# An unused 128 B tile behind the constants of a Mamba-2 scan with a mixer, and a decay tile 128 B longer

## The chip, the cores and the metric

The kernel runs on one core of one Trainium2 chip. The metric is device time in microseconds of one execution. In the profile PE is TensorE (matrix products), PEld its weight loads, DVE is VectorE, ACT is ScalarE, POOL is GpSimd and SP is SyncE, which here only issues DMAs. SBUF is the on-chip memory: 128 partitions, and a tile has the same byte address in each of them. PSUM holds the results of matrix products.

## What is computed

The first half is a scan over chunks (Mamba-2 SSD): for each of 4 batches and 8 heads, a sequence of 768 steps with head size 32 and state size 16.

```python
for c in range(nc):                       # chunks along the sequence
    cum = cumsum(log(a)[chunk])
    M = einsum('bhin,bhjn->bhij', Cc, Bc) * exp(cum_i - cum_j) * causal
    y[chunk] = M @ xc + einsum('bhin,bhnd->bhid', Cc, state) * exp(cum)
    state = exp(sum) * state + einsum('bhjn,bhjd->bhnd', Bc * decay_from_j, xc)
```

Its output, laid out as (batch 4, sequence 768, model 256), goes through a mixer: `u = x + ((x.T @ U) @ V).T` with rank 32 along the sequence, and `out = u + relu(u @ w_ch1) @ w_ch2` with 1024 inner channels. Inputs x, a, B and C are fp32; U, V, w_ch1 and w_ch2 are 64-bit floats, which the kernel loads as pairs of 32-bit words and converts on the chip.

## The kernel before

**Work and order.** The scan is cut into 12 pairs: 4 batches by 3 blocks of 256 steps. The mixer works per batch, on three blocks of 256 positions each. There is no loop that sets the order: `PLANS`, a list of words written out by hand, names every step (`g` gram, `m` and `M` mask, `s` state, `u` update, `i`, `n`, `j` the scan's outputs, `p`, `x`, `a` the low-rank part, `S`, `f`, `e`, `h`, `d` the two large products), and `follow` (L963) issues them in that order, with `manual_schedule` (L156), so that each engine takes its instructions as they are written. The mixer of one batch runs between the scan steps of a later one.

**The large products.** A product in full precision is split into three cheaper ones: an operand is written as a rounded part ("near"), a rest ("far") and a combination of both. `split` (L761) makes the tiles `u0`, `u1` and `u2` from a block of the mixer's input; `first` (L796) and `second` (L803) multiply them by the weights `w1[0]`, `w1[1]`, `w1[2]`; `second` and `third` (L814) write the three parts of the rectified result into tiles called `words`; `down` (L854) multiplies these by `w2[0]`, `w2[1]`, `w2[2]`, and `rows` (L822) does the same for the last block with the roles of the two operands exchanged. All of them issue their products through one line, L772. The first two blocks of batch 0 use plain fp32 products instead (`plain`, L783). DVE operations go through a recording helper and all have line L169.

**Loads.** `load_bc` (L199) and `load_x` (L212) fetch the inputs of the scan, and `load_words` (L241) the weights, all issued on SP by `begin` (L194, L195). The tile `bc` holds, for each head, B of two blocks of 128 steps and then C for 256 steps. A partition gets B in runs of 64 B, C in runs of 128 B and x in runs of 128 B.

**Where tiles lie.** Tiles come from four SBUF pools opened at L123 to L126: `const` (constants, weights and the decay tables), `raw` (the tiles `bc`, `x` and `words`), `att` (the scan's tiles) and `mix` (the mixer's). They lie behind each other in this order, and within a pool the tags lie in the order of their first use, every tile rounded up to 32 B. So a longer tile pushes all that lies behind it. The addresses of the built program, in bytes from the start of a partition, and their remainder modulo 256:

| tiles (pool) | before | modulo 256 |
|---|---|---|
| w10 to w12, w1f, w20 to w22 (const) | 20608 and on | 128 |
| ident and most other constants (const) | 77952 and on | various |
| bc, x, words (raw) | 86720, 94912, 103104 | 192 |
| BC, T, Cm (att): scaled B and C, and their transposes | 152256, 156352, 162496 | 192 |
| own (att), 1408 B | 168640 | 192 |
| bd, M, S, Sm (att) | 170048, 172096, 180288, 182336 | 64 |
| yT, ytok, pT, o, u0, u1, u2 (mix) | 185408 to 223296 | 64 |

The tile `own` is used once, in `keep` (L376), where DVE multiplies the logarithms of the decays by a mask and sums them. The tile `settled` (L457) is the last one of the `const` pool.

Of the kernel before, what the change touches and what calls it, by code (L numbers as in the profile page):

```python
# [10 lines left out]
FP32 = mybir.dt.float32  # L11
# [63 lines left out]
def kernel(  # L75
# [28 lines left out]
    P = 128  # L104
    NB, NH, S, D = x.shape
# [13 lines left out]
    Q = 32  # L119
# [3 lines left out]
    const = ctx.enter_context(tc.tile_pool(name="const", bufs=1))  # L123
    raw = ctx.enter_context(tc.tile_pool(name="raw", bufs=4))
    att = ctx.enter_context(tc.tile_pool(name="att", bufs=2))
# [17 lines left out]
    def bank(tag, *dims):  # L143
        t = psum.tile([P, *dims], FP32, tag=tag, name=tag, bufs=BANKS[tag])
        if fills[0]:
            idle(t if len(dims) == 1 else t.rearrange(
                {2: "p a b -> p (a b)", 3: "p a b c -> p (a b c)"}[len(dims)]), fills[0])
        fills[0] = 0
        return t
# [101 lines left out]
    own = {}  # L251
# [124 lines left out]
    def keep(bs, tag="w"):  # L376

        n = bs.stop - bs.start
        d = bank(tag, n, NC, NH)
        nc.tensor.matmul(out=d, lhsT=after, rhs=la[:, bs], start=True, stop=False,  # L380
                         skip_group_check=True)
        nc.tensor.matmul(out=d[:, :, :NC - 1], lhsT=onward, rhs=la[:, bs, 1:], start=False,
                         stop=True, skip_group_check=True)
        nc.scalar.activation(FD[:, bs], d, AF.Exp)

        d = bank(tag, n, NC, 2, NH)
        nc.tensor.matmul(out=d[:, :, :, 0], lhsT=middle, rhs=la[:, bs], start=True, stop=True,
                         skip_group_check=True)
        for m, sl in ((high, slice(0, NC - 1)), (low[0], slice(1, NC))):
            nc.tensor.matmul(out=d[:, :, :NC - 1, 1], lhsT=m, rhs=la[:, bs, sl], start=False,  # L390
                             stop=True, skip_group_check=True)
        J = 2 * NC - 1
        own = att.tile([P, NB, J, NH], FP32, tag="own", name="own", bufs=1)[:, :n]
        vector.tensor_tensor(
            out=own, in0=d.rearrange("p b c v h -> p b (c v) h")[:, :, :J],
            in1=mine[:, None, None, :].to_broadcast(own.shape), op=ALU.mult)
        vector.tensor_reduce(out=kept[:, bs], in_=own, axis=mybir.AxisListType.X, op=ALU.add)
        nc.scalar.activation(kept[:, bs], kept[:, bs], AF.Exp)
# [56 lines left out]

    st = {}
    settled = const.tile([P, 1], FP32)  # L457
    behind = {"turn": 0, "first": []}
    yT, ytok = {}, {}

    def prep(k, c=0, n=2):

        b, q = pairs[k]
        if "BC" not in st.setdefault(k, {}):
            st[k]["BC"] = att.tile([P, 2, 2, NH, N], FP32, tag="BC", name="BC")
        for g in [slice(4) if n == 2 else slice(c, c + 1) if c < 2 else slice(2, 4)]:
            part = st[k]["BC"].rearrange("p i c h n -> p (i c) h n")[:, g]
            vector.tensor_tensor(
                out=part, in0=bc_sb[k].rearrange("p h i c n -> p (i c) h n")[:, g],
                in1=F[:, b, q].rearrange("p h i c -> p (i c) h")[:, g, :, None].to_broadcast(  # L470
                    part.shape), op=ALU.mult)
# [479 lines left out]
    def ytokens_of(k, v):  # L951
# [4 lines left out]
                 j=crossed, y=yout, t=ytokens, L=load, Q=lambda k, c: prep(k, c, 1),  # L956
                 E=lambda k, c: decayed(k, c, 1), O=ytokens_of,
                 V=lambda k, c, v: turn(k, c, 1, "wx"[v // 2], vector if v % 2 else None))
    whole = dict(c=convert, R=refined, A=lambda i: decays(every_batch, "w", [i]),
                 K=lambda n: keep(every_batch, "z"), F=fill,  # L960
                 v=lambda n: spread())

# [53 lines left out]
```

## Time and profile before

| what | value |
|---|---|
| time of 3 runs, median (lowest to highest) | 225.8 us (225.74 to 226.55) |
| the profiled execution's own time | 225.21 us |
| its span, first to last instruction | 223.5 us |
| granted TensorE clock | 0.999 |
| busy: PE, PEld, DVE, ACT, POOL | 214.7, 192.8, 163.7, 122.5, 6.5 us |
| DMA | 69345 packets, 14.61 MB |

The profile shows one execution. A group's row gives the engine, the operation, what it writes and reads with the shape, how many there are, their busy time and the mean duration of one. Matrix products are pipelined, so one lasts longer than the distance to the next; the distance is what counts for the time, and the timeline of PE shows it: rows with a start, a length and a number of products, where a row's start and the next one's start lie as far apart as its products take. The chain of waits follows the work that ended last back from the last instruction.

### The profile page before, as it was taken

The numbers are of one execution on the slowest core, as the hardware profiler recorded it, in microseconds if no ns is written. First come the engines' busy times: TensorE is split into PE (matmuls) and PEld (weight loads), VectorE is DVE, ScalarE is ACT, GpSimd is POOL, SyncE is SP. The second block draws the span as 40 slices with busy tenths as digits, with TensorE's granted clock in tenths as the row PEclk, the third lists the DMA queues.
The fourth block names the chain that finished last, engine by engine and source line by source line (L and its number), as shares of the span: only waits on it lengthen the run. The fifth ranks groups of instructions, "written<-read, shape, count | busy, mean of one in ns | idle before, by whom it ended". The sixth has DMA issues, their size and how long they took to land.

```text
span 223.5 us, 7716 instructions
## 1 busy us (share of the span) xinstructions
PE 214.7 (96%) x3374; PEld 192.8 (86%) x3374; DVE 163.7 (73%) x341; ACT 122.5 (55%) x275; POOL 6.5 (3%) x22
## 2 busy tenths in 40 slices
PE   7977899899999999999999999999999999999994
PEld 5846567678889988989999997899998999999994
DVE  3489899999997979688189748948881694917541
ACT  2335774879548655674675351678332357545431
POOL 4023000000000000000000000000000000000000
PEclk9999999999999999999999999999999999999999
DMA  5977899989850005032015010200000000000142
GB/s 86 130 124 130 157 153 229 236 218 154 113 78 4 0 3 94 3 66 81 6 23 73 3 47 3 100 3 1 3 0 3 3 0 0 4 0 0 50 141 94
DMA packets 69345, 14.61 MB, mean 65 GB/s; under 512 B 63616, under 2 KB 67520, under 8 KB 69312
## 3 DMA queue, kind: packets, MB, share of 16 engines
q1 hardware_dynamic: 69312, 14.13, 32.5%
q8 instruction: 26, 0.43, 0.8%
q14 instruction: 7, 0.06, 0.1%
HBM read 10.98 MB, written 3.15 MB: 63 GB/s over the span
## 4 chain that ended last, share of the span: by engine, by line
PE 84%; SPq 8%; DMA 4%; DVE 2%; issue 1%; DVEq 0%
PE x L772 36%; PE z L772 28%; SPq L195 8%; DMA words<-in_moe_w_ch_dram 2%; PE w L730 2%; PE x L652 2%; PE w L891 2%; PE x L527 2%; PE w L701 2%; PE z L676 2%; PE x L741 2%; PE x L676 2%; DMA words<-in_moe_U_dram 1%; PE w L495 1%; PE w L562 1%
## 5 line engine op out<-in xcount | busy, mean ns | idle before, releaser
L169 DVE SCALAR_TENSOR_TENSOR words<-words 128x512 fp32r<-128x512 f32 (+6 forms) x60 | 39.5, 673 | 8.8 <-PE x L772 4.3
L772 PE MATMUL x<-words,w 128*128 128x256 f32 x288 | 39.5, 282 | 0.0
L772 PEld LDWEIGHTS x<-words,w 128*128 128x128 f32 x288 | 35.9, 188 | 1.0 <-issue 0.8
L772 PE MATMUL z<-u,w 128*128 128x256 f32 x240 | 34.4, 282 | 0.0
L772 PE MATMUL x<-u,w 128*128 128x256 f32 x240 | 33.9, 283 | 0.0
L772 PEld LDWEIGHTS z<-u,w 128*128 128x128 f32 x240 | 30.5, 188 | 0.5 <-issue 0.2
L772 PEld LDWEIGHTS x<-u,w 128*128 128x128 f32 x240 | 30.4, 189 | 0.4 <-issue 0.2
L777 ACT ACTIVATE z<-z 128x512 f32<-128x512 f32 (+1 forms) x24 | 13.7, 572 | 15.8 <-PE z L772 15.6
L777 ACT ACTIVATE x<-x 128x512 f32<-128x512 f32 (+1 forms) x27 | 15.3, 572 | 10.4 <-PE x L772 10.3
L772 PE MATMUL z<-words,w 128*128 128x256 f32 x144 | 19.5, 282 | 0.0
L772 PEld LDWEIGHTS z<-words,w 128*128 128x128 f32 x144 | 17.8, 188 | 0.3 <-issue 0.2
L169 DVE SCALAR_TENSOR_TENSOR words<-x,words 128x512 fp32r<-128x512 f32 x20 | 13.7, 686 | 4.8 <-ACT words L812 4.7
L169 DVE SCALAR_TENSOR_TENSOR words<-z,words 128x512 fp32r<-128x512 f32 x20 | 13.7, 686 | 3.1 <-ACT words L812 3.1
L812 ACT ACTIVATE words<-x 128x512 fp32r<-128x512 f32 x20 | 11.9, 600 | 6.5 <-PE x L772 6.5
L812 ACT ACTIVATE words<-z 128x512 fp32r<-128x512 f32 x20 | 11.8, 597 | 5.1 <-PE z L772 5.0
L594 ACT ACTIVATE Sm<-S,slot 128x128 f32<-128x128 f32 (+1 forms) x18 | 6.1, 389 | 14.4 <-DVE S L169 14.4
L169 DVE SCALAR_TENSOR_TENSOR S<-S,kept,w 128x64 f32<-128x64 f32 x40 | 11.2, 280 | 2.5 <-PE w L562 0.8
L169 DVE TENSOR_TENSOR BC<-bc,F 128x512 f32<-128x512 f32 (+2 forms) x18 | 8.7, 509 | 3.2 <-ACT F L372 2.6
L169 DVE TENSOR_TENSOR yT<-x,yT 128x384 f32<-128x384 f32 (+1 forms) x15 | 9.2, 616 | 2.3 <-PE x L772 2.0
L169 DVE TENSOR_TENSOR M<-x,causal 128x256 int32<-128x256 int32 x24 | 9.0, 418 | 2.4 <-PE z L527 2.4
L169 DVE TENSOR_TENSOR u<-yT,u 128x512 fp32r<-128x512 f32 x10 | 6.9, 688 | 5.2 <-ACT u L766 5.2
L652 PE MATMUL z<-T,Sm 32*64 32x64 f32 x180 | 9.7, 236 | 0.3 <-DVE settled L169 0.3
(146 smaller groups left out, 390.6 us busy)
## 6 DMA issues: line engine op xcount, KB each, us to landing
words<-in_moe_w_ch_dram SPq DMA_DIRECT2D x7, 512.0 KB, 6.0
x<-in_x_dram SPq DMA_DIRECT2D x24, 128.0 KB, 3.4
out_dram<-o SPq DMA_DIRECT2D x8, 256.0 KB, 2.2
bc<-in_B_dram SPq DMA_DIRECT2D x24, 64.0 KB, 3.4
bc<-in_C_dram SPq DMA_DIRECT2D x12, 128.0 KB, 3.3
out_dram<-words SPq DMA_DIRECT2D x3, 256.0 KB, 2.6
words<-in_moe_w_ch_dram SPq DMA_DIRECT2D x2, 256.0 KB, 4.5
out_dram<-o SPq DMA_DIRECT2D x2, 128.0 KB, 1.7
```

Source lines behind the costliest of these rows:

```text
L169: self.last = call(*args, **kwargs)
L195: op = nc.sync.dma_start(**kwargs)
L527: nc.tensor.matmul(out=g[r][cols, c], lhsT=s["T"][rows, 0, c, cols], rhs=s["Cm"][rows, :, :, ts(2 * c + p, Q)].rearrange("r v t i -> r v i ...
L594: nc.scalar.activation(s["Sm"][:, sl, v], s["S"][:, sl, ts(v, D)], AF.Copy, scale=slot[:, v, None])
L652: product = nc.tensor.matmul(out=y[r // 2][p][ts(r % 2, H), c], lhsT=own[ts(r, Q)], rhs=s["T"][ts(r, Q), 1, :, ts(2 * c + p, Q)].rearrange ...
L676: product = nc.tensor.matmul(out=y[n][p][ts(i, Q), c], lhsT=x_sb[k][half, c, h], rhs=s["M"][half, h // 2, c, h % 2], start=fresh(k, n, p, ...
L701: nc.tensor.transpose(out=t[:, c, g], in_=yT[b][:, g, ts(2 * q + c, P)], identity=ident)
L730: nc.tensor.matmul(out=p[ts(q, Q)], lhsT=U_sb[:, c], rhs=ytok[b][:, c, ts(q // 2, P)], start=(c == 0), stop=(c == NC - 1), skip_group_chec ...
L741: nc.tensor.matmul(out=h[q][:, :VS], lhsT=pT[rows], rhs=V4[rows], start=True, stop=True, skip_group_check=True)
L772: nc.tensor.matmul(out=t, lhsT=lhsT, rhs=rhs, start=start, stop=True, skip_group_check=True)
L777: nc.scalar.activation(t, t, AF.Copy, scale=1.0 + EPS)
L812: nc.scalar.activation(gs[j, i][0], t, AF.Relu, scale=NEAR)
```

## The change

One constant tile that nothing reads or writes is allocated behind `settled`, and `own` is allocated with 384 elements per partition (1536 B) in place of 352 (1408 B), of which the first 352 are used as before.

```diff
@@ keep
         J = 2 * NC - 1
-        own = att.tile([P, NB, J, NH], FP32, tag="own", name="own", bufs=1)[:, :n]
+        own = att.tile([P, 3 * P], FP32, tag="own", name="own", bufs=1)
+        own = own[:, :n * J * NH].rearrange("p (b j h) -> p b j h", b=n, j=J)
         vector.tensor_tensor(
             out=own, in0=d.rearrange("p b c v h -> p b (c v) h")[:, :, :J],
             in1=mine[:, None, None, :].to_broadcast(own.shape), op=ALU.mult)
@@
     st = {}
     settled = const.tile([P, 1], FP32)
+    gap = const.tile([P, Q], FP32)
     behind = {"turn": 0, "first": []}
```

In the built program the pool `raw` and, of `att`, BC, T, Cm and `own` start 128 B later than before; bd, M, S, Sm and the whole pool `mix` start 256 B later; `const` stays. Modulo 256, then, `raw`, BC, T, Cm and `own` go from 192 to 64, and everything else keeps its remainder. The list of instructions on every engine, their order, their semaphores, the slot that each tile takes and the PSUM addresses are the same in both programs.

## The prediction

> **What bounds the kernel now.** I read the page's busy times and chain first, since the change touches every engine's addresses and none of its instructions: what matters is which engine passes a longer operand on to the end.
>
> ```profile
> PE 214.7 (96%) x3374; PEld 192.8 (86%) x3374; DVE 163.7 (73%) x341; ACT 122.5 (55%) x275; POOL 6.5 (3%) x22
> ...
> PE 84%; SPq 8%; DMA 4%; DVE 2%; issue 1%; DVEq 0%
> ```
>
> TensorE is busy for 96% of the span and holds 84% of the chain; 36.0 and 28.2 points of that are the large products of L772. SP's issues and DMA make up 12% and lie at the start: in the chain's first 29.56 us SP issues B, C and x one behind the other (1.24 to 15.86 us), then come U (3.35 us) and a block of w1 (5.10 us). So there are two places where an address can cost time: the loads up to 30 us, and the pace of the large products after that. DVE and ACT are not on the chain to speak of, but would be with slower operands.
>
> **The change part by part.** It adds no instruction, wait or DMA and removes none. It moves tiles: `raw` (bc, x, words) and BC, T, Cm and own go from 192 to 64 modulo 256; bd, M, S, Sm and all of `mix` move by 256 B and keep their remainder. If a duration depended on the place of an operand, the trace of before would show it, since it holds both remainders already: tiles at 192, at 64, and constants at 128.
>
> *DVE and ACT.* Rows with the same operation and shape, at different remainders, by group with shapes kept apart:
>
> ```profile
> L169 DVE SCALAR_TENSOR_TENSOR words<-words 128x512 fp32r<-128x512 f32 x40 | 27.7, 692 | 8.8 <-PE x L772 4.3 <-PE z L772 3.1
> L169 DVE SCALAR_TENSOR_TENSOR u<-u,u 128x512 fp32r<-128x512 f32 x10 | 6.9, 692 | 1.4 <-PE z L772 1.1
> L169 DVE SCALAR_TENSOR_TENSOR w<-words,w 128x512 fp32r<-128x512 f32 x8 | 5.5, 692 | 0.3
> ```
>
> All operands at 192, all at 64, and a mix of 192 and 128: 692 ns each time. ACT's copies of 128x512 take 589 ns into o (64) and 594 to 611 ns into words (192, 4 of them): at most 22 ns by place, and not on the chain. I take 0 for DVE and ACT; the bound is 4 copies times 22 ns, 0.1 us either way.
>
> *Small products.* T, Cm and x are read in runs of 128 B at every multiple of 128 B from their start, so that a shift of 128 B exchanges the two halves of their products: as many start at 192 as before. 0. BC is read whole as weights of the transposes (L495, 276 ns each), as yT at 64 is (L701, 274 ns): 2 ns times 48, 0.1 us at most.
>
> *Large products.* The mean duration is 282 ns for x<-words and z<-u and 283 ns for x<-u, but the timeline shows that their distance is not one number:
>
> ```profile
> 117.79 1.07 PE L772 MATMUL z<-u,w 128*128 128x256 f32 x8
> 118.70 0.62 PE L772 MATMUL x<-u,w 128*128 128x256 f32 x4
> 119.15 1.57 PE L772 MATMUL z<-words,w 128*128 128x256 f32 x12
> 120.56 0.60 PE L701 MATMUL w<-ident,yT 128*128 128x128 f32 x4
> ```
>
> 8 with u take 118.70 - 117.79 = 0.91 us, 114 ns each; 12 with words take 120.56 - 119.15 = 1.41 us, 117.5 ns each. Over the trace there are 900 distances between neighbouring products of this kind with no wait in them: 247 of 113 or 114 ns, 653 of about 118 ns, a difference of 4.4 ns. With words streamed, 88% take 118 ns; with u streamed, 63%; with w2 streamed and words as weights, 12%. Relative to the weights at 128, words lies at +64, u at -64, and w2 against words at -64 too. After the change words would lie at -64, as u does. That is the one sign that speaks for an effect. Against it stand the exceptions:
>
> ```profile
> 212.13 1.98 PE L772 MATMUL z<-words,w 128*128 128x256 f32 x16
> 213.95 0.60 PE L891 MATMUL w<-ident,yT 128*128 128x128 f32 x4
> ```
>
> ```profile
> 150.33 2.52 PE L772 MATMUL x<-u,w 128*128 128x256 f32 x20
> 152.69 0.64 PE L772 MATMUL z<-u,w 128*128 128x256 f32 x4
> ```
>
> 16 with words take 1.82 us, 114 ns each, and 20 with u 2.36 us, 118 ns each; the same pair of u0 and w10 addresses comes back for other blocks with 113 ns one time and 118 ns another. So neither pace belongs to an address; it holds on for a stretch and changes where the streamed tile changes. I take 0. The bounds: all 653 steps of 118 ns brought to 113, 653 x 4.4 ns = 2.9 us less; the 247 others brought to 118, 1.1 us more. A rule of the Trainium skill bears on this: "SBUF — State Buffer", section "Who interferes with whom", says that TensorE and ScalarE never wait for anyone in SBUF; by it an address changes nothing in the pace, and the sum stays at 0, while by the rows above it could be -2.9 us.
>
> *Loads.* C's runs of 128 B start at 192 + 128, that is at 64 modulo 256 before, inside one block of 256 B; after, they start at 192 and reach over a border of 256 B, all of them. x's runs start at 192 and 64 by turns, before and after: half of them cross already. B's runs of 64 B never do. Time from issue to landing:
>
> ```profile
> x<-in_x_dram SPq DMA_DIRECT2D x24, 128.0 KB, 3.4
> ...
> bc<-in_B_dram SPq DMA_DIRECT2D x24, 64.0 KB, 3.4
> bc<-in_C_dram SPq DMA_DIRECT2D x12, 128.0 KB, 3.3
> ```
>
> x and C move 128 KB in 1024 runs each; half crossing or none differ by 0.1 us, so that all crossing costs 0.2 us at most. The packets say less still: 128 B ones take 13 ns each, from the 5th to the 95th percentile, those of x among them. Six of the 12 C loads are issued before 30 us, where SP is on the chain: 0 to 6 x 0.2 = 1.2 us. I take 0, by the packets. The weights' runs of 1024 B and more start off a border at 192 as at 64: 0. If the cover of PE's work went, the later six C loads (to 115.6 us) would add another 1.2 us; they are issued well ahead of use, and DVE waits 0.6 us in all for any bc.
>
> The sum is 0 on the profiled execution's 225.21 us (span 223.5 and 1.7 around it). That execution is 0.6 us under the median of the three, 225.8, and all four lie between 225.2 and 226.6; I forecast the median.
>
> **The rivals.**
>
> *Faster: words takes u's place at the weights, and its pace.* For it speaks the order 88, 63, 12% above and that a stretch with u at 114 ns turns to 118 ns with the first product of words, as at 119.15 us. If the 404 steps with words only took u's share, they would gain 404 x (0.88 - 0.63) x 4.4 ns = 0.4 us, hardly to be seen. If the distance of 113 ns then also held on from u to words, it would reach from all steps with words, 404 x 0.88 x 4.4 ns = 1.6 us, to all 653, 2.9 us: 222.9 to 224.2 us. It is beyond 0.5% if over 260 steps change. Against it: words at 114 ns and u at 118 ns in the same trace.
>
> *Slower: C's runs across a border of 256 B.* Its place is SP's chain up to 30 us, where transfers follow each other with DMA engines 80% busy over the first 30 us; the price is at most 0.2 us for each of six loads, 1.2 us: 227.0 us. It would be seen from 0.19 us each on. Against it stands x, which crosses with half its runs at the same 13 ns a packet. The Trainium skill has a rule for it: "DMA: Bandwidth & Descriptors", section "How a descriptor splits into AXI transactions", says that a descriptor goes out in transactions that start on 256 B borders, with bytes ahead of it moved for nothing. By that an unaligned C run would need 10 beats of 32 B in two transactions where it now needs 6 in one, if writes go as the reads that the page speaks of; the trace, with 13 ns for x's crossing and plain runs alike, does not show it.
>
> *Slower by the pace:* the stretches of 113 ns with u, or those of w2 with words (which goes to +64), are lost: up to 1.1 us, 226.9 us, for the same reason as above with the sign turned.
>
> *The change doesn't do what it says:* the shift could be lost in rounding. The addresses of the built program exclude it: 86720 becomes 86848, 185408 becomes 185664.
>
> **How the numbers follow.** No effect, 225.2 to 226.6 us: 0.60. Faster by the pace of the products: 0.24, of which 0.22 is beyond 0.5% (1.1 us, about what a measurement of this kernel can tell from no change). Slower by C's loads: 0.10, of which 0.09 beyond 0.5%. Slower by the pace: 0.06, about all of it near its end. So faster 0.22, same 0.64, slower 0.14. The predicted time is 225.8 us. The range takes the whole of no effect, about half of the faster case (from 223.8 us) and nearly all of the slower ones (to 227.0 us).
>
> **What would show it.** Right: the L772 rows keep 282 ns, the share of 118 ns distances stays near 653 of 900 with words near 88%, C lands after 3.3 us, the words block of w1 that the chain takes at 24.44 us starts there again. Faster: in PE's timeline the stretches with words have 114 ns. Slower: C's landing above 3.4 us and the first product of L772 on the chain, at 35.63 us now, later by as much as the span. Wrong altogether: a DVE or ACT row of 128x512 with another mean.

## The result and the profile after

The changed kernel takes 224.62 us (median of 21 runs, 222.74 to 226.01), the kernel before 225.74 us (21 runs, 224.42 to 227.81). The ratio is 0.9941, 95% interval 0.9916 to 0.9967: faster by 0.6%, 1.3 us. The forecast was no change; the range held the time. Here and below, ratios and intervals leave out the few executions that lie over 1.5% above the fastest of their kernel.

The two profiled executions last 225.21 and 223.32 us, with spans of 223.5 and 221.6 us. First the page of the changed kernel: busy times, and the chain by engine. L772 is L774 here, all lines behind L456 lie two further on.

```profile
PE 213.2 (96%) x3374; PEld 191.4 (86%) x3374; DVE 163.5 (74%) x341; ACT 122.3 (55%) x275; POOL 6.5 (3%) x22
...
PE 88%; SPq 7%; DMA 1%; DVE 1%; issue 1%; ACT 0%; DVEq 0%
```

DVE, ACT and POOL are where they were within 0.2 us; TensorE has lost 1.5 us of busy time with the same 3374 products. The groups of DVE with 128x512 elements, as the prediction showed them:

```profile
L169 DVE SCALAR_TENSOR_TENSOR words<-words 128x512 fp32r<-128x512 f32 x40 | 27.7, 692 | 8.5 <-PE x L774 4.1 <-PE z L774 3.0
L169 DVE SCALAR_TENSOR_TENSOR u<-u,u 128x512 fp32r<-128x512 f32 x10 | 6.9, 692 | 1.3 <-PE z L774 0.9
L169 DVE SCALAR_TENSOR_TENSOR w<-words,w 128x512 fp32r<-128x512 f32 x8 | 5.5, 692 | 0.3
```

Still 692 ns: in these rows the shift by 128 B changes nothing for DVE. The timeline of TensorE, at the same place in the order as the four lines of before:

```profile
117.07 1.07 PE L774 MATMUL z<-u,w 128*128 128x256 f32 x8
117.98 0.62 PE L774 MATMUL x<-u,w 128*128 128x256 f32 x4
118.43 1.53 PE L774 MATMUL z<-words,w 128*128 128x256 f32 x12
119.80 0.60 PE L703 MATMUL w<-ident,yT 128*128 128x128 f32 x4
```

12 with words now take 119.80 - 118.43 = 1.37 us, 114 ns each, where they took 117.5; u keeps 114. The stretch of 20 with u, 118 ns each before:

```profile
149.58 2.43 PE L774 MATMUL x<-u,w 128*128 128x256 f32 x20
151.85 0.62 PE L774 MATMUL z<-u,w 128*128 128x256 f32 x4
```

2.27 us, 113.5 ns each, though u has its old remainder. And near the end, where w2 is streamed and words are the weights, first before, then after:

```profile
218.49 1.07 PE L772 MATMUL x<-w,words 128*128 128x256 f32 x8
219.39 1.07 PE L772 MATMUL z<-w,words 128*128 128x256 f32 x8
```

```profile
216.51 1.10 PE L774 MATMUL x<-w,words 128*128 128x256 f32 x8
217.46 1.10 PE L774 MATMUL z<-w,words 128*128 128x256 f32 x8
```

8 in 0.95 us, 119 ns each, where they took 219.39 - 218.49 = 0.90 us, 112.5 ns each. So this kind went the other way. Of the 900 distances, 217 are longer than 114 ns, where 653 were; nearly all of these lie between 116 and 120 ns and are called the 118 ns pace below, those of 113 and 114 ns the 113 ns pace. The shares at 118 ns: words 22% (88% before), u 20% (64%), w2 with words 93% (17%). (The prediction's 63% for u and 12% for w2 count from 116 ns on, its 653 from 115.) Last, the loads, from issue to landing:

```profile
x<-in_x_dram SPq DMA_DIRECT2D x24, 128.0 KB, 3.8
...
bc<-in_B_dram SPq DMA_DIRECT2D x24, 64.0 KB, 3.6
bc<-in_C_dram SPq DMA_DIRECT2D x12, 128.0 KB, 4.3
```

C needs 1.0 us more, x 0.4 and B 0.2. The first large product of the chain begins at 36.07 us, 35.63 before.

The account of the 1.9 us between the spans: 0.44 us later into the large products (in this execution the granted TensorE clock also stood at half for 3.4 us from 24.3 us on, in that of before it did not); then 185.53 in place of 187.87 us, 2.34 less. Of these the 900 distances give 104.9 - 103.0 = 1.9 us. A stall of TensorE at 43.13 us, 0.65 us of "issue" in the chain of before, is missing after and gives about 0.9 us with what stood around it; the stretches of small products take 0.5 us more (40.3 in place of 39.8 us from the first large one on), in which there is one gap of 0.69 us between two products, at 141.31 us, that the trace of before lacks. The stall came back in the second profile of the same changed kernel (e8, 1.52 us at 46.46 us), so it belongs to an execution and not to the change.

### The profile page after: what moved, and what is told of

It is laid out like the page before. It is cut to its first block, busy times and chain, and to the rows that moved or that the text cites. A ratio compares the mean times of both kernels' runs of the same rounds, so it can differ in the third digit from the quotient of the medians.

```text
span 221.6 us, 7716 instructions
## 1 busy us (share of the span) xinstructions
PE 213.2 (96%) x3374; PEld 191.4 (86%) x3374; DVE 163.5 (74%) x341; ACT 122.3 (55%) x275; POOL 6.5 (3%) x22
## 4 chain that ended last, share of the span: by engine, by line
PE 88%; SPq 7%; DMA 1%; DVE 1%; issue 1%; ACT 0%; DVEq 0%
PE x L774 36%; PE z L774 28%; SPq L195 6%; PE x L654 3%; PE x L529 2%; PE w L732 2%; PE w L703 2%; PE w L893 2%; PE x L678 2%; PE z L678 2%; PE w L497 2%; PE x L743 2%; DMA words<-in_moe_U_dram 1%; PE w L564 1%; PE z L654 1%
## 5 line engine op out<-in xcount | busy, mean ns | idle before, releaser
L774 PE MATMUL x<-words,w 128*128 128x256 f32 x288 | 38.5, 280 | 0.0
L774 PEld LDWEIGHTS x<-words,w 128*128 128x128 f32 x288 | 35.0, 188 | 1.0 <-issue 0.8
L774 PE MATMUL z<-u,w 128*128 128x256 f32 x240 | 34.0, 281 | 0.0
L774 PE MATMUL x<-u,w 128*128 128x256 f32 x240 | 33.3, 281 | 0.0
L774 PEld LDWEIGHTS z<-u,w 128*128 128x128 f32 x240 | 30.1, 188 | 0.5 <-issue 0.2
L774 PEld LDWEIGHTS x<-u,w 128*128 128x128 f32 x240 | 29.9, 188 | 0.4 <-issue 0.2
L779 ACT ACTIVATE z<-z 128x512 f32<-128x512 f32 (+1 forms) x24 | 13.7, 572 | 15.4 <-PE z L774 15.2
L774 PE MATMUL z<-words,w 128*128 128x256 f32 x144 | 19.3, 281 | 0.0
L774 PEld LDWEIGHTS z<-words,w 128*128 128x128 f32 x144 | 17.6, 188 | 0.3 <-issue 0.2
L169 DVE SCALAR_TENSOR_TENSOR words<-x,words 128x512 fp32r<-128x512 f32 x20 | 13.7, 686 | 4.1 <-ACT words L814 4.1
L169 DVE SCALAR_TENSOR_TENSOR words<-z,words 128x512 fp32r<-128x512 f32 x20 | 13.7, 684 | 2.8 <-ACT words L814 2.8
```

Source lines behind the costliest of these rows:

```text
L169: self.last = call(*args, **kwargs)
L774: nc.tensor.matmul(out=t, lhsT=lhsT, rhs=rhs, start=start, stop=True, skip_group_check=True)
L779: nc.scalar.activation(t, t, AF.Copy, scale=1.0 + EPS)
```

## The experiments

Theory A: the pace of the large products is set by where the streamed tile starts against the weights, modulo 256 B; 64 (words before) holds it at 118 ns, 192 (u, and words after) leaves it free. With the weights at 128, a tile at 192 has the difference 64 and a tile at 64 the difference 192; for words, u and w2 the numbers below are differences, for bc and the other tiles they are addresses modulo 256. Theory B: the absolute start of the streamed tile sets it. Theory C: any shift does, or chance. Against the gain stands C's crossing of 256 B borders. "Pace" is below the number of the 900 distances that are longer than 114 ns, counted in the one profiled execution of each run; percentages are shares of such distances; the difference is (start of the streamed tile - start of the weights) modulo 256.

**e1, everything but the constants by 256 B.**

```diff
+    gap = const.tile([P, 64], FP32)      # behind settled; own as before
```

> The unused constant tile is 256 B and the decay tile has its old length: raw, att and mix all lie 256 B further, every remainder modulo 256 is that of the kernel before. Theory A (the pace of the large products is set by where the streamed tile starts against the weights, modulo 256): nothing changes, ratio 1.000 within 0.3%, about 650 of the 900 distances at 118 ns, words near 88%, C lands after 3.3 us. Theory C (any shift of the layout, or modulo 512, changes the pace): like the changed kernel, ratio near 0.994 and about 220 of 900.

Ratio 1.0002 (0.9966 to 1.0038). Pace 713 of 900, words 96%, u 70%; C lands after 3.1 us. A shift that keeps the remainders changes the time by less than 0.4% and leaves the pace near that of before: theory C falls, and modulo 512 with it.

**e2, the longer decay tile alone.** words stays at difference 64, u goes there from 192.

```diff
+        own = att.tile([P, 3 * P], FP32, tag="own", name="own", bufs=1)   # no gap
```

> Only the decay tile is longer, by 128 B: raw, BC, T and Cm stay at 192, while bd, M, S, Sm and mix (u among them) go from 64 to 192. Theory A: u now lies at +64 against the weights like words, so that u as well as words take 118 ns in 85% of the distances or more, over 750 of 900, about 0.6 us more than before, ratio 1.002 to 1.005; w2 streamed against words stays at 113 ns; C lands after 3.3 us. Theory C: the time and the pace move without regard to which tile moved, and words and u keep their difference.

Ratio 1.0039 (1.0007 to 1.0070). Pace 803: u 96% (64% before), words 88%, w2 with words 26%. The timeline of e2:

```profile
148.95 1.10 PE L773 MATMUL z<-u,w 128*128 128x256 f32 x8
149.89 0.63 PE L773 MATMUL x<-u,w 128*128 128x256 f32 x4
150.36 1.57 PE L773 MATMUL z<-u,w 128*128 128x256 f32 x12
151.77 2.40 PE L773 MATMUL x<-u,w 128*128 128x256 f32 x19
```

8 with u in 0.94 us and 12 in 1.41 us, 117.5 ns each: u takes on the pace of words when it takes on the difference. But 64 does not exclude 113 ns. One chain of e2 has it in u and words alike, up to its end at 128.49 us:

```profile
122.50 1.61 PE L773 MATMUL z<-u,w 128*128 128x256 f32 x12
123.95 1.52 PE L773 MATMUL z<-words,w 128*128 128x256 f32 x12
125.31 0.62 PE L773 MATMUL z<-u,w 128*128 128x256 f32 x4
```

12 with words take 125.31 - 123.95 = 1.36 us, 113 ns each.

**e3, the unused tile of 128 B alone.** words to 192, u to 64.

```diff
+    gap = const.tile([P, 32], FP32)      # own as before
```

> Only the unused constant tile of 128 B: raw, BC, T and Cm go to 64, and bd, M, S, Sm and mix (u among them) go to 192. Theory A: words at -64 has the 113 ns, u at +64 the 118 ns, the two exchange their parts: words under 40% at 118 ns, u over 80%, together 500 to 600 of 900, 0.2 to 0.7 us less by the pace, 0.4 us more by C's loads (landing 4.3 us as in the changed kernel), ratio 0.998 to 1.002. Theory C: words and u change alike.

Ratio 1.0087 (1.0054 to 1.0120), outside what was expected. Pace 749: u 96%, words 74% and not under 40%, w2 with words 31% though it lies at 64. So u is held at 64 again, but words at 192 gained little: most stretches of words follow one of u at 118 ns, and most of those stay there (18 of 22 that follow u without a break). The distances are 0.5 us longer in sum than before; the rest of the loss of 2.0 us is put down to C's crossing (landing 4.4 us), dearer than the 0.4 us that was allowed for it.

**e4, e11 and e14, the changed kernel with bc left at 192.** The unused tile lies between bc and x; words, u and weights have the addresses of the changed kernel, C does not cross.

```diff
         if k not in x_sb:
+            if not x_sb:
+                raw.tile([P, 32], FP32, tag="gap", name="gap", bufs=1)
             x_sb[k] = raw.tile([P, 2, NH, D], FP32, tag="x", name="x")
...
-    gap = const.tile([P, Q], FP32)       # of the changed kernel
```

> As the changed kernel, but the unused tile lies in raw between bc and x, so that bc alone stays where it was, at 192, and C's runs do not cross a border of 256 B. Theory A with a cost of C's crossing: pace as in the changed kernel (near 217 of 900 at 118 ns), C lands after 3.3 us and not 4.3, and the first large product comes 0.4 us earlier than in the changed kernel: ratio 0.991 to 0.993, ahead of both kernels. If crossing costs nothing and the later start has another reason: as the changed kernel, 0.994, with C's landing at 4.3 us.

> The kernel with bc left in place once more: words, u and weights have the addresses of the changed kernel, whose pace came back with 217 and 191 of 900, while this one had 523. Theory A with a pace at 192 that hangs on what went before in an execution: another number, anywhere from 190 to 550. If bc's place or the missing crossing of C sets it: 523 again within 60. The time: ratio 0.993 to 0.998.

> Words at 64 and bc at 192, next to the changed kernel on the same chip: by the two terms (pace 1 to 2 us less, no crossing) ratio 0.987 to 0.994, 0.4 to 1.2 us ahead of the changed kernel. If the crossing is covered: as the changed kernel within 0.3%.

Ratios 0.9959 (0.9930 to 0.9988), 0.9868 (0.9820 to 0.9916) and 0.9932 (0.9895 to 0.9968). C lands after 3.1, 3.2 and 3.2 us. Pace 523, 174 and 415 in the three profiles of one and the same kernel. So the difference 192 does not fix the pace; it leaves it open, and one execution has three times as many distances of 118 ns as another. e4 gained less than expected (0.991 to 0.993) and e11 more. This version is ahead of the kernel before: each interval lies below 1. In e4 that is not firm, since the mean of all its executions is 0.9992 of that of the kernel before (0.9877 in e11, 0.9937 in e14). On the chip that it shared with the changed kernel (e15) it was at 0.9932 against 0.9988, two intervals that overlap. The timeline of e11:

```profile
118.40 1.53 PE L775 MATMUL z<-words,w 128*128 128x256 f32 x12
119.77 0.60 PE L704 MATMUL w<-ident,yT 128*128 128x128 f32 x4
```

1.37 us for 12 with words, 114 ns each, as in the changed kernel.

**e5, the constants moved too.** The unused tile lies ahead of all constants: every absolute start moves by 128 B, the differences stay.

```diff
+    ahead = const.tile([P, 32], FP32)
     a_sb = const.tile([NB * NH * NC // 2, 2, P], FP32)
```

> The unused tile of 128 B lies ahead of all constants, so that everything moves by 128 B together: the weights of the large products go from 128 to 0, words from 192 to 64, u from 64 to 192, and their differences stay. Theory A (the difference sets the pace): the pace of the kernel before, u near 0.65 and words near 0.88 at 118 ns, about 650 to 710 of 900. Theory B (the absolute start of the streamed tile sets it): the exchange that the unused tile of 128 B behind the constants alone gave, u near 0.96 and words well below it. In both C crosses and lands after 4.3 us, 0.4 us lost at the start: ratio 1.001 to 1.005.

Pace 650, words 88%, u 64%, w2 with words 17%: the kernel before had 653 with 88, 64 and 17%. Theory B falls. The ratio is 1.0074 (1.0041 to 1.0106), more than expected. In the profile it lies ahead of the large products, which start at 38.81 us, with C at 4.1 us; but this execution also had half the clock for 17 us there, so the profile alone does not split the loss.

**e6, e7, e9 and e10, other differences.** The decay tile is the longer one; the unused tile has 192, 64, 160 and 96 B, which puts words and u alike at 128, 0, 96 and 32, and so at the differences 0, 128, 224 and 160.

```diff
+    gap = const.tile([P, 48], FP32)      # e6; 16 in e7, 40 in e9, 24 in e10
```

> Unused tile of 192 B and the longer decay tile: words, u and w1, w2 all start at 128, difference 0 in all three kinds of large products, w2 against words too. Theory A: the three kinds have the same share of 118 ns, since none comes from a stretch of another difference; either near 0 (104.0 us less 2 us, ratio 0.990) or near 1 (ratio 1.005), with no mixture by kind. A rival (the kind of tile, words or u, sets the pace and not the place): u and words differ as before, 0.64 and 0.88. C and x start at 128 and do not cross a border of 256 B: C lands after 3.1 to 3.3 us, x sooner than 3.4 us.

> Unused tile of 64 B and the longer decay tile: words and u start at 0, the weights at 128, difference 128 in all three kinds. Theory A: one share of 118 ns for all kinds, near 0 or near 1. As for difference 0 neither C nor x cross a border of 256 B. If difference 0 and 128 have the same pace, only the sign at 64 matters; if one is at 113 ns throughout, it is the better layout, with a ratio near 0.990.

> Unused tile of 160 B and the longer decay tile: words and u start at 96, the weights at 128, difference 224 (32 B below the weights) in down and in the products of u, 32 in rows. So far the mean distance was 119.8 ns at difference 0, 117.7 at 64, 118.8 at 128, and between 113.3 and 116.2 at 192. Theory A (a matter of the difference alone, with the range around 192 free): as at 192 or better, under 220 of 900 at 118 ns, ratio 0.990 to 0.996. If the free range ends between 192 and 256: over 800 of 900 and a ratio above 1.004. C crosses a border here (its runs start at 224).

> Unused tile of 96 B and the longer decay tile: words and u start at 32, the weights at 128, difference 160 (96 B below the weights). Between 192 (free at times) and 128 (118.8 ns): if the pace goes gradually with the difference, about half of the 900 at 118 ns and a mean near 116; if it is a border, either under 220 or over 800. C crosses a border here (its runs start at 160).

| run | difference of words and u | pace | mean distance, u and words | ratio (95%) | C lands |
|---|---|---|---|---|---|
| e6 | 0 | 891 of 898 | 119.8 and 119.8 ns | 1.0138 (1.0100 to 1.0176) | 3.2 us |
| e7 | 128 | 881 | 118.7 and 118.9 ns | 1.0085 (1.0049 to 1.0122) | 3.2 us |
| e9 | 224 | 889 of 899 | 118.2 and 118.3 ns | 1.0104 (1.0065 to 1.0142) | 4.3 us |
| e10 | 160 | 900 | 117.8 and 118.0 ns | 1.0095 (1.0061 to 1.0129) | 4.2 us |

The timeline of e6, at difference 0:

```profile
151.33 2.56 PE L774 MATMUL x<-u,w 128*128 128x256 f32 x20
153.73 0.65 PE L774 MATMUL z<-u,w 128*128 128x256 f32 x4
```

2.40 us for 20, 120 ns each. The same 20 with u took 2.36 us before and 2.27 us after. Of the six differences tried with u, only 192 gives it 113 or 114 ns in more than 4% of its distances; it is no matter of words or u, which have one pace at one difference. At 128, 160 and 224 the distances spread from 115 to 123 ns, so the mean says more there than the count. 224 was expected to be as free as 192 and is not; nor is 160. The ratio of e6, 3.1 us, is more than was expected of either outcome; its distances are 107.5 - 104.9 = 2.6 us longer than before.

**e8 and e15, the changed kernel again.**

> The changed kernel again, for how far its pace comes back: with the same addresses of words, u and weights the kernel with bc left in place had 523 of 900 distances at 118 ns, the changed kernel's own profile 217. Theory A with a pace that is open at -64 and held by what went before: anything from 200 to 550 of 900, words and u alike, ratio 0.992 to 0.997. If the place of bc had changed the pace: 217 again within 50.

> The changed kernel on the same chip: pace 1 to 2 us less, C's crossing 0.4 to 1.2 us more: ratio 0.993 to 0.998.

Ratios 0.9967 (0.9932 to 1.0002) and 0.9988 (0.9953 to 1.0022): in these two the gain is not clear of noise. C lands after 3.8 and 4.1 us. Pace 191 and 563 in the profiles: 217, 191 and 563 in three executions of one program. Even so, the seven profiles with the differences of the changed kernel (174 to 563) do not meet the four with those of the kernel before (653, and 713, 650 and 701 in e1, e5 and e13). One chain shows where two of these executions part, first in the profile of the result, then in e15:

```profile
173.13 1.98 PE L774 MATMUL z<-u,w 128*128 128x256 f32 x16
174.95 1.52 PE L774 MATMUL x<-words,w 128*128 128x256 f32 x12
176.31 1.07 PE L774 MATMUL z<-u,w 128*128 128x256 f32 x8
```

```profile
175.50 2.05 PE L774 MATMUL z<-u,w 128*128 128x256 f32 x16
177.39 1.58 PE L774 MATMUL x<-words,w 128*128 128x256 f32 x12
178.80 1.11 PE L774 MATMUL z<-u,w 128*128 128x256 f32 x8
```

12 with words take 1.36 us, 113 ns each, in the one and 1.41 us, 117.5 ns each, in the other, and so do nearly all products that follow in each, u and words, up to the chain's end at 200 and 204 us. To count this over the traces, call a stretch the products of one streamed tile that follow each other with no other product and no wait in between, and give it the pace of most of its distances. In the seven profiles with u and words both at 192, a stretch at 113 ns that is followed by the other tile stays at 113 ns every time (187 of 187), and one at 118 ns drops to 113 ns in 13 of 107. In the five in which the two differ (before, e1, e3, e5, e13), every stretch that follows from 192 to 64 goes at 118 ns, 111 of 111, 37 of them after 113 ns; from 64 to 192, 28 of 92 stretches at 118 ns drop to 113. So it is the passage from 192 to 64 that ends the better pace, and the change leaves no such passage between u and words.

**e12, bc, x and words alone.** The unused tile behind the constants, and another of 128 B ahead of BC: BC, T, Cm and own keep 192.

```diff
+    st, gaps = {}, []
...
+    gap = const.tile([P, 32], FP32)
...
         if "BC" not in st.setdefault(k, {}):
+            if not gaps:
+                gaps.append(att.tile([P, 32], FP32, tag="gap", name="gap", bufs=1))
```

> The unused tile of 128 B behind the constants and another of 128 B ahead of BC: bc, x and words go to 64, while BC, T, Cm and own keep 192 and the rest keeps its remainder. Theory A: words is what matters, so the pace and the time of the changed kernel: 190 to 550 of 900, ratio 0.992 to 0.998, C landing at 4 us or more. If the scan's BC, T and Cm brought the gain: the pace may change but the time stays at ratio 1.000 to 1.003, with the small products taking more than their 39.6 to 40.5 us.

Ratio 0.9964 (0.9935 to 0.9993), pace 408, small products 40.1 us, C at 4.1 us: the gain comes with bc, x and words moved alone, of which only words is an operand of the products in question; BC, T and Cm have no visible part in it.

**e13, bc alone.** The unused tile behind the constants, another of 128 B between bc and x: only bc goes to 64.

```diff
+    gap = const.tile([P, 32], FP32)
...
+            if not x_sb:
+                raw.tile([P, 32], FP32, tag="gap", name="gap", bufs=1)
```

> bc alone goes from 192 to 64 (an unused tile of 128 B behind the constants, another between bc and x): C's runs cross a border of 256 B, and every large product has the differences of the kernel before. If the crossing is a cost of its own at the start: the pace of before (600 to 720 of 900 at 118 ns), C lands after 4 us or more, 128 B packets at 14.0 to 14.5 ns in the mean, ratio 1.002 to 1.006 (0.4 to 1.2 us later into the large products). If the loads are covered: ratio 1.000 within 0.2% and the same landing.

Ratio 1.0066 (1.0037 to 1.0096), 1.5 us, with the pace of before (701; words 91%, u 72%). The landing in e13:

```profile
bc<-in_C_dram SPq DMA_DIRECT2D x12, 128.0 KB, 4.1
```

The packets of 128 B take 14.1 ns in the mean, 13.1 before. So the place of bc costs 1.5 us by itself (0.8 to 2.2 by the interval). A like price comes out of e15 and e14, one with the crossing and one without, on one chip: 0.9988 - 0.9932 = 0.0056, 1.3 us, though their intervals overlap. C's runs are not alone in it: in e13 x lands after 3.8 us in place of 3.4 and B after 3.6 in place of 3.4, x from the remainder it had before and B without crossing anything.

## Why the prediction was wrong

*What bounds the kernel:* right. Both terms that moved the time are the two places named, the loads up to 30 us and the pace of the large products.

*DVE, ACT, small products at 0:* right, 692 ns in all rows; the stretches of small products take 39.8 and 40.3 us, with the gap of 0.69 us in the second; e12 shows no effect of the scan's tiles.

*Large products at 0:* this is the step that failed. It was argued that "neither pace belongs to an address", since u and w10 at the same addresses came with 113 ns one time and 118 ns another. The observation was right and the conclusion was not. A difference of 192 allows both paces, one of 64 (and of 0, 128, 160, 224) makes the better one rare: the share of u at 118 ns went from 64 to 96% in e2 and e3, at 64, and to 98 to 100% at 0, 128, 160 and 224. The order 88, 64, 17% in the trace of before was the sign. Words at 64 with 114 ns (212.13 us before), the chain of e2 at 122.50 us and w2 with words in e3, with 31%, are true exceptions: at 64 a stretch can begin at 113 ns and last. The prediction also said that a pace "holds on for a stretch and changes where the streamed tile changes"; it did not ask which way. From u to words, from 192 to 64, it always went to 118 ns, and the change takes these passages away. What decides the pace of a chain's first stretch is open: for u and words at 192 it was 126 times 118 ns and 135 times 113, over the traces that have only 64 and 192. The rule of the Trainium skill that was weighed here ("SBUF — State Buffer", "Who interferes with whom": TensorE waits for no one) speaks of engines; read as the prediction read it, that the pace cannot depend on the place, it does not hold here: the mean distance of u went from 114.0 to 119.8 ns with the place alone. That the weight load and the stream, which run side by side in the trace, hinder each other is a likely reason, since it is their difference that counts (e5), but no run shows the two reads themselves.

*The rival "words takes u's place":* this is what happened. Its first price, 0.4 us, supposed that u would stay at 63%; u's own share fell too, to 20%, without a change in its place, since no words at 64 came in between to end its 113 ns. Its upper form, 1.6 to 2.9 us, is where the first profile lies with 1.9 us; the seven profiles with these differences have distances that are 0.5 to 2.1 us shorter in sum than before.

*Loads at 0:* failed too, with the other sign. "128 B packets take 13 ns" was the wrong row, because no C run crossed in it and x's crossing half does not show there. After, C lands 1.0 us later and not 0.2, and bc alone costs 1.5 us, where 1.2 was the bound and lies within the interval. The rule of the Trainium skill in "DMA: Bandwidth & Descriptors", section "How a descriptor splits into AXI transactions", says that a run that does not start on a border also costs the beats from the border below it, and speaks of reads; worked out in the prediction, it has the right sign for C. But by it x, half of whose runs cross, should gain when none do, and in e6, where none cross, the packets of 128 B take 12.97 ns in place of 13.08. Why crossing costs something with C and nothing with x is open.

*The sum:* two wrong zeros of opposite sign, about 1 to 3 us less by the pace (the ratios of e4, e14 and e11, with bc in place) and 1.3 to 1.5 us more by C, which left 1.3 us. That the range held the time is in part luck: the median of e11, without the second term, is 223.19 us, below the range.

The single executions scatter for a further reason: in all profiles but that of before the granted TensorE clock stands at half for 3 to 17 us somewhere between 14 and 32 us. Among the 21 of the changed kernel the four with a mean granted clock of 1.000 average 223.9 us, the five with 0.969 or 0.970 average 225.5 us. The first large product of a profile starts anywhere between 35.6 and 38.9 us, and ratios of many runs, not single profiles, carry the prices above. Profiles with equally long half-clock stretches can be compared, though: with 13.7 us of it the first large product starts at 37.4 to 37.7 us where C does not cross (e2, e4, e7, e14) and at 38.2 to 38.9 us where it does (e10, e12, e15). That is 1.0 us in the mean, another reading of C's price.

## What to carry to other kernels

When products with 256 columns follow each other with a weight load each, look at the distance between their starts in the timeline, not at their mean duration (280 to 283 ns here, before and after); two distances in one trace are a sign that the places of streamed tile and weights may matter, and a shift of one pool by 64 or 128 B is a cheap trial. A trace in which one place shows both paces and another place almost only the worse one is evidence for a dependence, not against it; look then at what happens where the streamed tile changes, and in which direction. Where a shift moves load buffers as well, price the loads apart from the products and move the two by separate gaps.

## What was not expected of the hardware

- The distance of two such products depends on the difference of the starts of streamed tile and weights modulo 256: in the mean 119.8 ns at 0, 117.7 at 64, 118.7 at 128, 117.8 at 160, 118.2 at 224, and 114.0 to 116.4 ns at 192 (u, one profile each or more).
- At 192 the pace is not settled by the program: 174 to 563 of 900 at 118 ns for equal addresses of words, u and weights (seven profiles).
- A pace lasts from stretch to stretch: with u and words both at 192, none of 187 stretches at 113 ns was followed by one at 118 ns without a break, while every one of 37 ended when the next tile lay at 64.
- With C's runs across a border of 256 B, C's loads land 0.5 to 1.1 us later than before (nine profiles); bc moved alone, they land 0.8 us later and the whole kernel takes 0.66% longer (0.37 to 0.96%).
